# Where the length-47 sets and the token output's quarters stand inside a tile of six channel pairs

## The chip, the cores and the metric

The kernel runs on one core of one Trainium2 chip. The metric is device time in microseconds of one execution, from the first to the last work on the core; the time of a kernel is the median over its runs. All arithmetic is in fp32.

## The reference

For each of 8 batches of 3008 positions and 256 channels, a global filter in the frequency domain comes first, and an MLP-mixer block (token mixing, then channel mixing) after it:

```python
X = np.fft.rfft(x, axis=1)
Y = X * (filt_r + 1j * filt_i)[None, :, :]
y = np.fft.irfft(Y, n=x.shape[1], axis=1)          # (8, 3008, 256)

xt = y.transpose(0, 2, 1)
h = np.maximum(xt @ w_tok1, 0.0) @ w_tok2          # 3008 -> 256 -> 3008
u = y + h.transpose(0, 2, 1)
h2 = np.maximum(u @ w_ch1, 0.0) @ w_ch2            # 256 -> 1536 -> 256
return u + h2
```

## The kernel before, in words

**The filter.** 3008 is 64 x 47. The transform is done in two stages, and back in two. The first stage (length 64) is a run of units over the 47 residues: `a_unit` in its plain form, `a_pair` in the form used from the third group on, which takes sums and differences (`x_sums`) first; its result goes to DRAM (`z_tmp`). The second stage works on 16 *length-47 sets* of two frequencies each: `b_pair` (a product with the table `wb`), `products` (two VectorE instructions that multiply by the filter's real and imaginary parts, straight from PSUM), `join` (two VectorE instructions that add the parts up) and `bi_pair` (the product back), whose result goes to DRAM (`g_tmp`). A set that follows another issues its own `b_pair`, then `bi_pair` of the set before it, then `products`. `b_pair` writes the PSUM banks `acc` and `b`; `bi_pair` writes the two banks `pg`, except for the last set's, which takes `acc` and `b`. After `products`, SP is given the loads for the set two further on (`t2_load`, `w_load`).

The batches go through the filter in groups: batch 0 alone, then (1, 2), (3, 4), (5, 6) and 7. Batch 0's filter runs first. Each other group's filter is woven into the mixer of earlier batches: group (1, 2) beside batch 0, group (3, 4) beside batches 1 and 2, group (5, 6) beside batches 3 and 4, batch 7 beside batches 5 and 6. Batch 7's mixer has no filter work beside it. `dft` is a generator that yields the kind of its next piece: `a` and `w` for first-stage units and the loads after them, `b` for a set, `m` for its join, `i` for the last `bi_pair`.

**The mixer.** `mix` walks over 8 batches x 6 tiles (`m`, 512 positions, the last 448) x 6 channel pairs (`jp`, 0 to 5). One channel pair is called a step here. A step's order on each engine is the program's order:

- TensorE: `up_first` (4 products, L941), then the first part of `down` of the step before (3 products, L975 with `hh`), then token work if any is due; the loop yields *place 0*. `up_last` (3 products, L957); *place 1*. `down`'s second part (2 products, L975 with `t`); *place 1.5*. Its third part (2 products); then `finish` or token work if due; *place 2*. Each fp32 product shows as two TensorE rows.
- VectorE (line L919 is the helper `v`): `up_middle` (`hh`, `s`), one piece of `todo_v` if there is one, `h_sums` of the step before (`t`, three instructions), then the token work's adds, after `up_last` the two `hh` adds, and again one piece of `todo_v`.

Filter pieces are put at the places where `mix` yields. A position is written as 3.2 for channel pair 3, place 2.

`todo_v` holds small VectorE jobs. When a tile's last `down` is issued (step 0 of the next tile, place 2), `finish` puts six there (`a`, `b_`, `c`, `d`, a transpose, a transpose and the store); two run at once and the others at 1.0, 1.1, 2.0 and 2.1. The store is 16 DMAs issued by POOL (L1022). Step 0's `up_first` of the next tile needs `v`, which `v_steps` makes in two jobs (`t13`, `t24`) as soon as that tile's `u` is there.

**The token output.** `u` of the next tile is made one tile ahead. For batch 0, `u_unit` does it in two products (one for each half of the channels). For other batches a seven-product form does it in four *quarters* (`u_quarter`, parts 0 to 3, lines L862 and L840), each in one of the banks `acc` and `b` in turn (`free_bank`); each is read by VectorE adds, and part 0 by a ScalarE copy too. The last part also queues the two `v_steps`, the load of the next weights (`w2m_load`, SP, L881) and lets the next batch's filtered rows be loaded (`t4_load`, SP, L750). The table `own` says at which position each part runs (first entry for batch 0, second for the others); `new`, which is for the last tile, is not touched. At step 32 of a batch the next batch's token sums are made (`token_product`).

**When a filter piece is due.** The main loop asks at each place whether the next piece is due: `a` and `w` at place 1 (three places a step beside batch 0), the rest by tables of positions. With these tables the sets beside batch 0 ran in steps 2, 3 and 5 of tile 1, 1, 2, 3 and 5 of tiles 2 and 3, and 0, 1, 2, 3 and 5 of tile 4, each with its join at place 2 of the same step. Beside later batches a set ran at 5.1.5 and at 2.1.5 (1.1.5 in the last tile), with joins at 0.1 of the next tile and at 3.0.

Of the kernel before, what the change touches and what calls it, by code (L numbers as in the profile page):

```python
# [42 lines left out]
JP = JT // 2  # L43
# [84 lines left out]
def kernel(  # L128
# [299 lines left out]
    def sum_up():  # L428
        while behind:
            behind.pop(0)()  # L430

    def convert():

        convert_middle()
        convert_end()

    def convert_middle():
        advance(middle)
        sum_up()

    def convert_end(copy_now=True):
        ended[0] += 1
        advance(end)
        if copy_now:
            copies()
        fill(5)
# [3 lines left out]
    def copies():  # L450

        while copied[0] < len(tiles) and copied[0] <= ended[0] + 1:
            advance(copy)
            copied[0] += 1
# [3 lines left out]
    def fill(ahead):  # L458
        while not pause and begun[0] < len(tiles) and begun[0] < ended[0] + (4 if begun[0] >= len(tiles) - len(LAST) else ahead):
            start()  # L460

    def start():
        advance(begin)
        begun[0] += 1
# [282 lines left out]
    def t4_load(b, c, lo=PARTS[0], hi=P, queue=nc.sync):  # L747
        if lo == 0:
            t4[b, c] = t4p.tile([P, TC4, D], FP32, tag="t4", name="t4")
        queue.dma_start(t4[b, c][lo:hi], rows_of(g_d, b)[lo:hi, ts(c, TC4), :])  # L750

    def token_sums(b):
        acc = bank(free_bank()).rearrange("p (t d) -> p t d", t=TC)
        for a in range(A):
            for t in range(TC):
                nc.tensor.matmul(acc[:, t, :], w1[:, a, ts(t, P)], t4[b, a // TC4][:, a % TC4, :],
                                 start=(a == 0 and t == 0), stop=(a == A - 1 and t == TC - 1))
        return acc
# [69 lines left out]
    def token_relu(b, acc):  # L828
        h1 = h1p.tile([P, TC, D], FP32, tag="h1", name="h1")
        nc.scalar.activation(out=h1, in_=acc, func=AF.Relu)  # L830
        return h1
# [198 lines left out]
    def u_part(b, m, i):  # L1030
        if i == 0:
            uts[b, m] = up.tile([P, DH, 512], FP32, tag="u", name="u")
        (u_quarter if b else u_unit)(b, m, h1s[b], uts[b, m], i)

    def v_steps(b, m):
        vts[b, m] = vp.tile([P, 4, 256], FP32, tag="v", name="v")
        t13, t2, t4_ = u_sums(uts[b, m], vts[b, m], width(m))

        def t24():
            t2()  # L1040
            t4_()

        return [t13, t24]
# [7 lines left out]
    def mix(next_ready):  # L1051
# [8 lines left out]
                wait.clear()  # L1060


        own = ({(4, 2): (0, 1)}, {(3, 0): (0,), (4, 0): (1,), (4, 2): (2, 3)})
        new = {(JP - 2, 0): (0, 1), (JP - 1, 0): (2, 3)}

        def u_parts(b, m, jp, place):
# [15 lines left out]
        n = MT * JP  # L1082
        for i in range(len(items) + 1):
# [11 lines left out]
            if now:  # L1095
                b, m, jp = items[i]
# [64 lines left out]
    with tc.manual_schedule():  # L1161
        nc.sync.dma_start(wa0, wa0_d)
        nc.vector.memset(turned[:, A:K2, :], 0.0)
        for t in filts:
            nc.vector.memset(t, 0.0)
        half = 0
        second = dft(GROUPS[1])
        for i, _ in enumerate(dft(GROUPS[0])):
            if i == 0:
                nc.scalar.dma_start(wai_t, wait_d)  # L1170
            k = i - NXC - 2

            if i < NXC:
                if i in (1, 3, 5, 7, 9):
                    start()
                if i == NXC - 1:
                    copies()
                    for t, src in ((wa, wa_d), (was, was_d), (wai, wai_d), (ident, ident_d)):
                        nc.scalar.dma_start(t, src)
            elif k >= 0:  # L1180
                if k == K2 - 5:
                    pause.append(True)
                while half < 2 * IN_B * (k + 1) // K2:
                    if half % 2:
                        convert_end()
                    else:
                        convert_middle()
                    half += 1

                if 19 <= k < 25:  # L1190
                    t4_load(0, k - 19, 0, PARTS[1])
                elif 26 <= k < 29:
                    for c in range(2):
                        t4_load(0, 2 * (k - 26) + c, PARTS[1], PARTS[2])
                elif k in (30, 31):
                    for c in range(3):
                        t4_load(0, 3 * (k - 30) + c, PARTS[2], PARTS[3])
        pause.clear()

        fill(5)  # L1200
        for c in range(A // TC4):
            t4_load(0, c, PARTS[3], P, (nc.sync, nc.gpsimd)[c % 2])
        both = wcp.tile([P, 2, JP, 7, P], FP32, tag="wc", name="wc")

        chan.extend((both[:, 0], both[:, 1]))
        next(second)
        for i in range(IN_B, A // 2 + TC * W2G):
            convert()
            if i == A // 2 + BY_PE - 1:
                sum_up()  # L1210
                acc = token_sums(0)

        ahead[0](XF, nc.gpsimd)
        h1s[0] = token_relu(0, acc)
        for dh in range(DH):
            convert()
            u_part(0, 0, dh)
        for f in v_steps(0, 0):
            f()
        convert_end(False)  # L1220
        for _ in range(XB):
            next(second)
        group, todo, done = -1, iter(()), True

        def next_ready(b):
            return done or b != GROUPS[group][-1]

        coming = "a"  # L1230
        n = MT * JP
        for b, i, place in mix(next_ready):
            if group + 1 < len(GROUPS) and b == GROUPS[group + 1][0]:
                if not done:
                    raise AssertionError("the filter's steps don't fit beside the mixer's")
                group += 1
                done = group + 1 == len(GROUPS)
                todo = iter(()) if done else dft(GROUPS[group + 1]) if group else second
                coming = "a"
            if done:  # L1240
                continue
            jp = i % JP
            if coming in "aw":
                due = place == 1 or group == 0 and place != 1.5
            elif group:
                due = (jp, place) in {"b": ((5, 1.5), (1 if i >= n - JP else 2, 1.5)), "m": ((0, 1), (3, 0)), "i": ((1, 0), (3, 2))}[coming]
            else:
                due = (jp - (coming == "i")) % JP in ((5, 1, 2, 3) if i < 4 * JP else (5, 0, 1, 2, 3)) and place == {"b": 1.5, "m": 2, "i": 0}[coming]
            if coming == "a" and group == 0 and i < JP - 1:
                due = {0: 2, 1: 0, 1.5: 0, 2: 1}[place]  # L1250
            for _ in range(due):
                if not done:
                    coming = next(todo, "end")
                    done = coming == "end"
# [30 lines left out]
```

## Time and profile before

| | |
|---|---|
| median of 5 runs | 2460.81 us (2459.18 to 2461.69) |
| profiled execution | 2460.81 us, its span 2459.0 us |
| mean granted TensorE clock | 0.996 |
| busy: TensorE, VectorE, ScalarE, GpSimd (POOL) | 2394.9, 1942.4, 686.4, 619.9 us |
| DMA moved | 278.66 MB, mean 113 GB/s |

Busy time is the union of the instructions of an engine in the one profiled execution. A row of the timeline gives the start in us from the span's start, the duration, the engine, the line of the program, the operation, the tiles it writes and reads, the shape, a count of merged instructions, and in brackets the idle time before it with what ended it. A row of the waits gives who waited for whom: us in total, times, and the longest. A row of the windows gives the stretch, its length, the busy time and instructions of TensorE, its weight loads, VectorE, ScalarE and POOL, then the granted clock, the DMA share and GB/s.

### The profile page before, as it was taken

How to read it: one execution, taken by the hardware profiler on the slowest of the kernel's cores; microseconds unless marked ns; L12 is line 12 of the kernel's file. 1: busy time of each engine (PE TensorE's matmuls, PEld its weight loads, DVE VectorE, ACT ScalarE, POOL GpSimd, SP SyncE). 2: the span in 40 equal slices, each digit the busy share in tenths (PEclk: the TensorE clock that was granted, in tenths of full speed). 3: DMA queues.
4: the chain of work that ended last, by engine and by line, in shares of the span. 5: the costliest groups of instructions: out<-in, count | busy, mean ns of one | idle time of the engine just before them, and what ended most of it. 6: DMA issues, size and time to landing. Idle time of an engine off the chain costs nothing.

```text
span 2459.0 us, 35588 instructions
## 1 busy us (share of the span) xinstructions
PE 2394.9 (97%) x12340; PEld 1979.7 (81%) x12340; DVE 1942.4 (79%) x3684; ACT 686.4 (28%) x1355; POOL 619.9 (25%) x1115
## 2 busy tenths in 40 slices
PE   7999999999999999999999999999999999999998
PEld 4756666978788877987888878897889888898887
DVE  7797788787887788778877887877787788777776
ACT  5733223133222222123222222213221222212222
POOL 7486322122112211211211122112112112112121
PEclk8999999999999999999999999999999999999999
DMA  9985445553442232545333322433324121411100
GB/s 218 243 233 167 155 133 175 161 158 111 116 141 79 82 91 66 171 128 157 92 123 114 92 72 76 160 96 119 96 77 151 46 75 46 146 65 30 39 15 20
DMA packets 187420, 278.66 MB, mean 113 GB/s; under 512 B 35485, under 2 KB 125291, under 8 KB 187240
## 3 DMA queue, kind: packets, MB, share of 16 engines
q1 hardware_dynamic: 140952, 212.56, 28.4%
q0 software_dynamic: 34688, 53.83, 8.1%
q10 hardware_dynamic: 11600, 10.00, 1.3%
q8 instruction: 98, 1.61, 0.3%
q14 instruction: 82, 0.67, 0.1%
HBM read 193.52 MB, written 82.72 MB: 112 GB/s over the span
## 4 chain that ended last, share of the span: by engine, by line
PE 42%; DVE 8%; issue 1%; ACT 0%; SPq 0%; DMA 0%; DVEq 0%; ACTq 0%; POOL 0%
PE ps_po L975 16%; PE ps_pg L941 9%; PE ps_pg L957 6%; PE ps_acc L862 2%; PE ps_b L807 2%; DVE t L919 2%; DVE u L919 2%; PE ps_b L862 1%; PE ps_acc L807 1%; PE ps_b L523 1%; DVE hh L919 1%; DVE s L919 1%; PE ps_pg L523 1%; PE ps_b L840 1%; PE ps_acc L840 1%
## 5 line engine op out<-in xcount | busy, mean ns | idle before, releaser
L1022 POOL DMA_DIRECT2D out_dram<-r x752 | 407.9, 550 | 1653.6 <-ACT hh L962 931.3
L962 ACT ACTIVATE hh<-hh 128x512 f32<-128x512 f32 (+1 forms) x576 | 347.9, 621 | 1086.8 <-DVE hh L919 1086.8
L919 DVE TENSOR_TENSOR hh<-ps_pg,s 128x512 f32<-128x512 f32 (+3 forms) x864 | 482.8, 587 | 212.0 <-ACT s L944 210.9
L975 PE MATMUL ps_po<-t,wc 128*128 128x256 f32 (+1 forms) x2304 | 559.7, 381 | 19.5 <-DVE t L919 18.4
L975 PEld LDWEIGHTS ps_po<-t,wc 128*128 128x128 f32 x2304 | 423.9, 190 | 154.1 <-issue 55.4
L941 PE MATMUL ps_pg<-v,wc 128*128 128x256 f32 (+1 forms) x1728 | 413.5, 375 | 1.4 <-POOL wc L381 1.3
L975 PE MATMUL ps_po<-hh,wc 128*128 128x256 f32 (+1 forms) x1728 | 413.4, 375 | 1.3 <-POOL wc L382 0.8
L941 PEld LDWEIGHTS ps_pg<-v,wc 128*128 128x128 f32 x1728 | 326.8, 190 | 42.2 <-DVE v L919 3.1
L975 PEld LDWEIGHTS ps_po<-hh,wc 128*128 128x128 f32 x1728 | 327.4, 190 | 40.7 <-POOL wc L382 2.0
L957 PE MATMUL ps_pg<-u,wc 128*128 128x256 f32 (+1 forms) x1152 | 294.6, 378 | 5.2 <-DVE hh L919 3.9
L919 DVE TENSOR_TENSOR t<-t,hh 128x256 f32<-128x256 f32 (+1 forms) x576 | 245.8, 427 | 19.8
L957 PEld LDWEIGHTS ps_pg<-u,wc 128*128 128x128 f32 x1152 | 215.4, 190 | 47.4 <-DVE hh L919 22.4
L919 DVE TENSOR_TENSOR s<-ps_pg,hh 128x512 f32<-128x512 f32 (+1 forms) x288 | 196.1, 681 | 30.7 <-DVE hh L919 0.9
L919 DVE TENSOR_TENSOR t<-hh 128x512 f32<-128x512 f32 (+1 forms) x288 | 194.9, 677 | 0.6 <-ACT hh L962 0.6
L944 ACT COPY s<-ps_pg 128x256 f32<-128x256 f32 (+1 forms) x288 | 106.0, 368 | 312.0 <-PE ps_pg L941 309.1
L941 PE MATMUL ps_pg<-u,wc 128*128 128x256 f32 (+1 forms) x576 | 169.9, 377 | 5.2 <-DVE hh L919 5.2
L957 PE MATMUL ps_pg<-v,wc 128*128 128x256 f32 (+1 forms) x576 | 168.8, 375 | 0.0
L941 PEld LDWEIGHTS ps_pg<-u,wc 128*128 128x128 f32 x576 | 107.0, 190 | 25.5 <-DVE hh L919 11.1
L919 DVE TENSOR_TENSOR u<-ps_acc,u 128x256 f32<-128x256 f32 (+1 forms) x84 | 46.2, 550 | 95.3 <-PE ps_acc L862 86.7
L957 PEld LDWEIGHTS ps_pg<-v,wc 128*128 128x128 f32 x576 | 108.7, 190 | 13.1
L919 DVE TENSOR_TENSOR u<-ps_b,u 128x512 f32<-128x512 f32 (+2 forms) x126 | 74.5, 591 | 28.9 <-PE ps_b L862 26.7
L677 DVE TENSOR_TENSOR p<-ps_b,filt 128x1024 f32<-128x1024 f32 (+1 forms) x64 | 69.8, 1091 | 29.8 <-PE ps_pg L523 26.1
(152 smaller groups left out, 2667.7 us busy)
## 6 DMA issues: line engine op xcount, KB each, us to landing
w<-w_tmp SPq DMA_DIRECT2D x84, 448.0 KB
w<-w_tmp SPq DMA_DIRECT2D x35, 896.0 KB
out_dram<-r POOLq DMA_DIRECT2D x696, 32.0 KB, 3.3
t<-g_tmp SPq DMA_DIRECT2D x42, 512.0 KB
g_tmp<-t SPq DMA_DIRECT2D x96, 192.0 KB
t<-z_tmp SPq DMA_DIRECT2D x180, 96.0 KB
z_tmp<-t SPq DMA_DIRECT2D x60, 256.0 KB
filt<-in_x_dram SPq DMA_DIRECT2D x90, 128.0 KB
```

The costliest lines, as they stand in the source:

```text
L523: nc.tensor.matmul(outs(i, j), stat(i, j), mov(i, j), start=True, stop=True)
L677: nc.vector.tensor_tensor(out=prods[c, h], in0=pss[h].unsqueeze(1).to_broadcast([P, 2, nb, D]), in1=filts[c % FB][:, :, 0, :].unsqueeze(2) ...
L807: nc.tensor.matmul(ps[:, at], w[:, n], mov, start=(j == 0 and i in (0, 2)), stop=(j == AP - 1 and i >= 5))
L840: nc.tensor.matmul(ps[:, ds(q * P, n)], t4[b, c][:, r, ts(dh, P)], wai[:, 0:n], start=(first and q == 0), stop=(not first and q == 3))
L862: nc.tensor.matmul(ps[:, ds(j * hw, hw)], h1[:, n, :], w2m[m % 2][:, at, 0:hw], start=(i < 2 and j == 0), stop=(j == len(todo) - 1))
L919: nc.vector.tensor_tensor(out=out, in0=in0, in1=in1, op=op)
L941: nc.tensor.matmul(ps[:, 0:hw], chan[0][:, jp, n, :], mov, start=True, stop=True)
L944: nc.scalar.copy(out=s[:, 0], in_=g[0][:, 0, 0:hw])
L957: nc.tensor.matmul(ps[:, 0:hw], chan[0][:, jp, n, :], mov, start=True, stop=True)
L962: nc.scalar.activation(out=hs, in_=hs, func=AF.Relu)
L975: nc.tensor.matmul(po[i][:, j, 0:hw], chan[1][:, jp, n, :], mov, start=(jp == 0 and first == 1), stop=(jp == JP - 1 and last == 1))
L1022: q.dma_start(bass.AP(tensor=ob.tensor, offset=ob.offset + row * D + g * cw, ap=[[N1 * D, 32], [D if h else -D, n], [1, cw]]), blocks[ts(g ...
```

## The change

Two tables of positions and one condition change; no instruction is added or taken away.

- Sets beside batches 1 to 6 run at 1.1.5 and 4.1.5 of every tile (the second and the fifth channel pair), their joins at 3.1 and 5.1. The last set's way back is due at 0.0 or 3.2.
- Sets beside batch 0 run in steps 2, 3, 4 and 5 of a tile (the third to the sixth channel pair).
- The token output: in batch 0 the two halves run at 3.0 and 4.0, both at 4.2 before. In the others parts 0 and 1 run at 3.0, part 2 at 3.2 and part 3 at 4.0; before, part 0 ran at 3.0, part 1 at 4.0 and parts 2 and 3 at 4.2. So `v_steps` run at 4.1 and 5.0, where they ran at 5.0 and 5.1.

```diff
-        own = ({(4, 2): (0, 1)}, {(3, 0): (0,), (4, 0): (1,), (4, 2): (2, 3)})
+        own = ({(3, 0): (0,), (4, 0): (1,)}, {(3, 0): (0, 1), (3, 2): (2,), (4, 0): (3,)})
...
             elif group:
-                due = (jp, place) in {"b": ((5, 1.5), (1 if i >= n - JP else 2, 1.5)), "m": ((0, 1), (3, 0)), "i": ((1, 0), (3, 2))}[coming]
+                due = (jp, place) in {"b": ((1, 1.5), (4, 1.5)), "m": ((3, 1), (5, 1)), "i": ((0, 0), (3, 2))}[coming]
             else:
-                due = (jp - (coming == "i")) % JP in ((5, 1, 2, 3) if i < 4 * JP else (5, 0, 1, 2, 3)) and place == {"b": 1.5, "m": 2, "i": 0}[coming]
+                due = (jp - (coming == "i")) % JP in (2, 3, 4, 5) and place == {"b": 1.5, "m": 2, "i": 0}[coming]
```

## The prediction

> **What bounds the kernel now.** I read the page first: busy shares, then the waits.
>
> ```profile
> span 2459.0 us, 35588 instructions
> ...
> PE 2394.9 (97%) x12340; PEld 1979.7 (81%) x12340; DVE 1942.4 (79%) x3684; ACT 686.4 (28%) x1355; POOL 619.9 (25%) x1115
> ```
>
> TensorE has work in 97% of the span, and the change neither adds nor removes a matmul. Only idle TensorE time can move: 64.1 us, of which the first 90 us hold 17. TensorE's own waits say for whom it idles later:
>
> ```profile
> PE ps_po L975 <- DVE t L919: 18.4, 36, 0.6
> ```
>
> The matmuls of the down product wait for VectorE's sums t. To see where, I took step lengths from the timeline (start of one first L941 row to the next; a step is one channel pair). Steps 0 to 5 of a tile of batch 7, which has no filter work: 6.12, 6.40, 6.05, 6.90, 9.99, 6.05 us. A tile of batch 2 (from 822.18), with sets in steps 2 and 5: 6.05, 7.15, 8.12, 6.91, 9.99, 8.12. So a set costs 8.12 - 6.05 = 2.07, and step 1, which holds no set, is 0.75 longer than in the bare tile. The windows of the two tiles agree: 46.3 - 41.5 = 4.8, against 2 x 2.07 = 4.14.
>
> ```profile
> 822.20:868.50 46.30, 45.69 (x231) 37.11 (x230) 38.38 (x69) 12.35 (x25) 8.66 (x16) 1.00 0.27 80
> ...
> 2246.90:2288.40 41.50, 41.38 (x199) 36.20 (x199) 31.53 (x62) 10.23 (x21) 8.66 (x16) 1.00 0.13 36
> ```
>
> The timeline of step 1 shows why. First the bare tile (step 1 begins at 2253.06), then the tile with sets (828.23):
>
> ```profile
> 2252.39 0.68 DVE L919 TENSOR_TENSOR u<-ps_po,u 128x512 f32<-128x512 f32 x1
> ...
> 2256.83 0.69 DVE L919 TENSOR_TENSOR t<-hh 128x512 f32<-128x512 f32 x1
> ```
>
> ```profile
> 828.16 0.69 DVE L683 TENSOR_TENSOR p<-p,p 128x512 f32<-128x512 f32 x1
> ...
> 828.76 0.69 DVE L919 TENSOR_TENSOR u<-ps_po,u 128x512 f32<-128x512 f32 x1
> ...
> 832.75 0.68 DVE L919 TENSOR_TENSOR t<-hh 128x512 f32<-128x512 f32 x1
> ...
> 833.58 0.45 PE L975 MATMUL ps_po<-t,wc 128*128 128x256 f32 x1 [0.59 <-DVE t L919]
> ```
>
> The end of a tile (finish: u from ps_po) starts 0.67 before step 1 when VectorE is free, and 0.53 after it when the set's joining (two adds, 0.60 each until the next can start) stands ahead in step 0. t comes 3.77 and 4.52 after step 1's start: the 0.75.
>
> **The change, part by part.** The profiled execution took 2460.81, its span 2459.0 plus 1.8 around it; that is also the median of the five runs (2459.18 to 2461.69). About 0.2% (4.9 us) is what a measurement of this kernel can tell from no change.
>
> *Sets in steps 1 and 4, joins in 3 and 5 (batches 1 to 6).* Step 0 loses its join, so step 1 falls to the bare tile's 6.40 plus the set. A set in step 1 has a row: step 31 of batch 1 (719.0), where the switch to the set and its second half cost 0.10 more than in step 2. Gain per tile with two full sets: 0.75 - 0.10 = 0.65. Is VectorE free by step 0? In step 4 the third quarter's add (0.69) and t13 (0.69) lie before the products (2 x 1.22), which wait for the set's matmuls anyway, about 1.2 later. Products end where the next hh can start (843.84 + 1.21 against 845.03), so step 5 starts undelayed. There t24 (0.43 + 0.43, in a row) now stands before t: hh at 1.53 after the step's start, s to 2.74, t24 to 3.54, t to 4.14, plus 0.14 (833.44 to 833.58) = 4.28, against 4.32 when TensorE gets there. I take 0; bounds: no gain, because t moves later, and 0.7 per tile, from batch 0's step at 384.84 where hh starts 1.2 late. The join in step 5 ends at 7.47; step 0's hh is due at 6.05 + 1.53 = 7.58. Covered.
> Steps 1 with a set before them now: per pair group, batches 1 and 2 (3 and 4 alike): 7.54, 7.16, 8.95 (w 448, set inside) and 7.14, 4 x 7.16. Against 6.40, or 5.98 in the last tile, plus 0.10: 1.03 + 0.65 + 0.78 + 0.65 + 2.6 = 5.7. Two groups: 11.4. The last group has half-width sets (step 1 at 6.62): 0.12 each, 1.1 with its last tile.
> Step 33 of batch 1 (752.2) takes 6.41 and its next 7.13, in batch 2, without a join, 5.30 and 7.02: the join at 3.0 delays the adds that free ps_pg. At 3.1 it follows them, and step 34's quarters cover it: 1.2 + 1.2 + 0.6 = 3.0. But step 35 loses its set, which hid t24 ahead of the next batch's first step (0.25 in batch 3's step 0, 0 in batch 2's): -0.75 for three.
>
> *Quarters 0, 1 at 3.0, 2 at 3.2, 3 at 4.0.* The same 14 rows of L862 and 16 of L840, shifted. The first-stage units (a_pair) beside batches 1, 3 and 5 waited 0.2 for quarter 1's adds in step 4; now they do in step 3: even. Their fetch of w (L881) and of t (L750) moves half a step forward on SP, ahead of a set's loads needed two sets later: nothing. t24 half a step earlier removes the 0.07 at step 0 of five bare tiles: 0.4.
>
> *A price at the last set.* Its second half runs at 3.2 on the banks acc and b (16th set, batches 2, 4, 6). Now quarter 2 precedes it there, and its first bank is quarter 2's: the add on that bank ends 0.2 + 0.69 + 0.13 after the quarter. Against a 0.1 switch: 0.9, three times: -2.7. Bounds: 0 each, if the other bank comes first, and 1.2, if the join's two adds (0.60 each) stand ahead of it.
>
> *A price at the first set.* It moves from step 17 to step 16 of its group (step 10 for the last group): it must be ready at 6.05 + 9.51 + 6.58 = 22.14 after step 14 starts (1172.2). Its inputs are late for a reason that the change leaves alone:
>
> ```profile
> 1179.47 8.66 POOL L1022 DMA_DIRECT2D out_dram<-r  x16 [39.88 <-ACT hh L962]
> 1188.12 1.47 POOL L697 MEMSET filt<- 128x512 f32 x3
> ```
>
> ```profile
> 1188.69 0.33 SPq L226 DMA_DIRECT2D filt<-in_filt_r_dram  x1
> ...
> 1191.62 0.30 SPq L631 DMA_DIRECT2D t<-z_tmp  x1
> ...
> 1195.39 0.36 SPq L632 DMA_DIRECT2D t<-z_tmp  x1
> ```
>
> POOL issues 16 stores before it clears the filter tiles; only then SP issues eight filter loads and eight of t. The DMA windows show the first filter bytes about 1 us after their issue, so I take 1.2 to landing: 1195.39 + 0.36 + 1.2 = 1196.9, wanted by the set's second half at 1194.35 + 0.47. Lost: 2.1; in batches 1 and 5 (last issue at 612.81, 1727.72) 1.2 and 1.3. Sum -4.6; bounds -2 (landing 0.4 after issue) and -8 (whole set waits, landing 1.9).
>
> The Trainium skill speaks against the change more strongly here: "DMA: Bandwidth & Descriptors", section "Anatomy of one DMA — SWDGE (gpsimd) path", gives a DMA a fixed cost of about 2 us. By that an estimate of the three waits is some 2 us higher in all; these SP loads are of the other path, and no row tells the landing of these loads.
>
> *Batch 0: sets in 2, 3, 4, 5, joins in the same steps at place 2; the two token products at 3.0 and 4.0.* Here the join stands before the next hh:
>
> ```profile
> 386.99 0.68 DVE L683 TENSOR_TENSOR p<-p,p 128x512 f32<-128x512 f32 x1
> 387.59 0.42 DVE L919 TENSOR_TENSOR hh<-ps_pg,s 128x256 f32<-128x256 f32 x1
> ...
> 390.05 1.13 PE L975 MATMUL ps_po<-t,wc 128*128 128x256 f32 x4 [0.42 <-DVE t L919]
> ```
>
> A step after a set loses 0.5 to 1.3 unless something fills it. Steps 12 to 17 took 6.50, 9.41, 9.30, 8.71, 11.67, 8.12 = 53.7, where six bare steps, four sets and the token products (5.2) make 49.7: 4.0 lost; 18 to 23 lose 4.4; 24 to 29 lose 7, as a set in step 0 puts its join behind finish (11.44 in step 25); 8 to 11 lose 2.1. Now the products (2.6 each) come before the wait in steps 3 and 4, where TensorE's time covers the join: 0 lost. Step 2 follows a step without a set: 0.05 (step 8). Step 5 meets t24 after a late hh: 1.4 (step 14's 1.2 plus 0.2 for t24 over the transpose). Step 0: 0.5 (step 12); step 1: 1.2 (step 13's without its set). 3.15 a tile, three times, plus 1.5 and 0.3: 11.2 against 17.3. Gain 6; bounds 2 and 9. In tile 0, VectorE is the bound (10.4 of 10.4 us in step 3); half of the token products moves into its shadow: 1.0, bounds 0 and 2.
>
> **Sum.** 11.4 + 1.1 + 3.0 - 0.75 + 0.4 - 2.7 - 4.6 + 6 + 1 = 14.85 less: 2446.0.
>
> **Rivals.**
> 1. *VectorE is late in step 5 and t24 makes it worse* (slower). Mechanism: products from step 4 spill past 1.53 of step 5, then t24 and t follow. It decides when what precedes the products in step 4 grows by over 1.2 us. hh then starts 1.2 late and TensorE waits 1.16 at each of 16 full and about 0.5 at each of 8 half sets: 22.6 lost, 2446.0 + 22.6 = 2468.6. Against it: the rows of step 4 sum to the 1.2 to spare.
> 2. *The wait in step 1 stays*, since the set now stands in step 1 itself (8.95 at step 31 speaks for it, though a join preceded that one): 11.4 and 1.1 fall away, 2458.5, no change.
> 3. *The change in the groups does what it says, and the first set is not late*, since the loads land sooner and POOL's 16 issues end earlier: 4.6 and part of the last set's 2.7 back: 2440.
>
> **How the numbers follow.** Forecast 0.55 (2440 to 2453 by the bounds: batch 0 -4/+3, first sets -3.4/+2.6, step 5 at half its bound for some tiles); rival 3 0.2; rival 2 0.13; rival 1 0.08; anything else slower 0.04. The range 2437 to 2460 takes in rivals 2 and 3 and leaves out rival 1 and a little at each end. Faster: 0.55 + 0.2 + 0.03 of rival 2 = 0.78; same: the 0.1 left of rival 2; slower: 0.08 + 0.04 = 0.12.
>
> **What would show it.** Right: step 1 of batch 2 at 8.5 (6.40 + 2.07 + 0.10) with a hh 1.9 to 2.0 after its start; step 5 at 6.05; the tile 45.7 long; step 16 of batches 1, 3 and 5 with TensorE idle 1 to 2 us before the first set; step 27 of batches 2 and 4 some 0.9 longer. Wrong: rows "PE ps_po <- DVE t" in step 5, or step 1 at 9.2. Batch 0 is right if its steps 3 and 4 take 10.7 each and step 1 about 7.2.

## The result, and the profile after

The changed kernel takes 2456.07 us (median of 23 runs, 2451.14 to 2460.98) where the kernel before took 2461.07 (44 runs, 2458.49 to 2464.03): ratio 0.9978, 95% interval 0.9973 to 0.9984. It is 5.0 us faster; 14.85 was forecast. The profiled execution took 2457.73 us, its span 2456.0. Two of the twelve executions of experiment 6's kernel took 5575 and 14191 us for an unknown reason; its median counts them, its ratio does not.

The page's first lines and TensorE's longest wait, after:

```profile
span 2456.0 us, 35551 instructions
...
PE 2396.7 (98%) x12340; PEld 1987.3 (81%) x12340; DVE 1951.5 (79%) x3684; ACT 686.6 (28%) x1355; POOL 621.0 (25%) x1115
```

```profile
PE ps_po L975 <- DVE t L919: 10.8, 18, 1.6
```

The matmul count is the same, and the wait for t fell from 18.4 to 10.8. Yet busy TensorE time grew by 1.8 us with nothing added: some rows ran at a lower clock. The step lengths place the time. Stages are cut at step starts, and the forecast's terms are put into the stage that each belongs to:

| stage | before | after | change | forecast |
|---|---|---|---|---|
| up to batch 0's step 3 | 169.1 | 171.8 | +2.7 | 0 |
| steps 3 to 7 (first tile) | 50.9 | 54.7 | +3.7 | -1.0 |
| steps 8 to 29 (sets beside batch 0) | 203.0 | 197.7 | -5.3 | -6.0 |
| steps 30 to 35 | 58.0 | 57.9 | -0.1 | 0 |
| batches 1 and 2 | 581.8 | 578.1 | -3.7 | -4.55 |
| batches 3 and 4 | 581.8 | 582.4 | +0.6 | -3.65 |
| batches 5 and 6 | 561.0 | 560.4 | -0.7 | +0.75 |
| batch 7 | 253.4 | 253.0 | -0.4 | -0.4 |

Changes are taken before rounding. The first row is before anything that the change moves: of the kernels below, the ten that leave those steps alone too reached that step between 168.2 and 173.2. So its 2.7 is no effect of the change, and with it the profiled gain is 3.1 where the medians give 5.0.

The steady tiles went as forecast. The windows of the tile of batch 2 from 821.30 and of the bare tile of batch 7, after:

```profile
821.30:867.00 45.70, 45.58 (x231) 37.20 (x230) 38.70 (x69) 12.39 (x25) 8.67 (x16) 1.00 0.29 81
2244.22:2285.65 41.43, 41.31 (x199) 36.23 (x198) 31.63 (x61) 10.24 (x21) 8.67 (x16) 1.00 0.13 36
```

The steps of the first are 6.04, 8.60, 6.04, 9.53, 9.45, 6.04. The timeline of step 1 (from 827.35), VectorE's rows first:

```profile
826.68 0.68 DVE L919 TENSOR_TENSOR u<-ps_po,u 128x512 f32<-128x512 f32 x1
...
831.12 0.68 DVE L919 TENSOR_TENSOR t<-hh 128x512 f32<-128x512 f32 x1
```

```profile
831.95 1.10 PE L975 MATMUL ps_po<-t,wc 128*128 128x256 f32 x4
832.98 0.65 PE L523 MATMUL ps_b<-t,wb 48*64 48x512 f32 x2
```

Finish starts 0.67 before the step, t at 3.77 as in the bare tile, and the down product on t starts with no wait in brackets. The set follows it directly.

Two places did not go as forecast, and a third did. At the first set of batch 3 (step 16 begins at 1185.12) the inputs are late; GpSimd's, SP's and TensorE's rows of the timeline:

```profile
1176.79 8.66 POOL L1022 DMA_DIRECT2D out_dram<-r  x16 [39.87 <-ACT hh L962]
1185.43 1.47 POOL L697 MEMSET filt<- 128x512 f32 x3
```

```profile
1186.00 0.33 SPq L226 DMA_DIRECT2D filt<-in_filt_r_dram  x1
...
1192.87 0.36 SPq L632 DMA_DIRECT2D t<-z_tmp  x1
```

```profile
1193.11 1.43 PE L523 MATMUL ps_b<-t,wb 48*64 48x512 f32 x4 [1.32 <-DMA t<-z_tmp]
1194.38 2.38 PE L523 MATMUL ps_acc<-t,wb 48*64 48x512 f32 x4
1196.68 2.07 PE L975 MATMUL ps_po<-t,wc 128*128 128x256 f32 x4
1198.55 1.06 PE L941 MATMUL ps_pg<-u,wc 128*128 128x256 f32 x2
1199.40 2.43 PE L941 MATMUL ps_pg<-v,wc 128*128 128x256 f32 x6
```

The chain is the one forecast: 16 stores, then the clears, then sixteen loads. But the six L941 rows took 2.43 us; in step 1 of the tile above six such rows took 1.46. The windows over that stretch give the granted clock in the third column from the right:

```profile
1190.00:1192.00 2.00, 1.79 (x9) 1.23 (x7) 1.83 (x4) 0.74 (x2) 0.00 (x0) 1.00 0.32 98
1192.00:1196.60 4.60, 3.49 (x8) 0.85 (x8) 1.64 (x2) 0.48 (x1) 0.00 (x0) 0.77 0.37 108
1196.60:1201.50 4.90, 4.90 (x13) 3.89 (x13) 1.65 (x2) 0.37 (x1) 0.00 (x0) 0.51 0.62 172
1201.50:1210.00 8.50, 8.50 (x41) 7.49 (x40) 7.62 (x15) 1.60 (x3) 0.00 (x0) 1.00 0.66 194
```

The clock records say half speed for 6.8 us from 1194.5. Steps 16 and 17 took 13.43 and 7.43; with inputs in time they take 8.59 and 6.04 (shown below). In batch 1 the same step took 10.51, in batch 5 9.97 (8.16 in time), without a lower clock.

The second place is step 5 of batch 0: 14.88 us, before 8.62. Rows of GpSimd, ScalarE and TensorE:

```profile
188.44 1.11 POOL L766 DMA_DIRECT2D w_tmp<-w  x1
189.55 1.03 POOL L767 DMA_DIRECT2D w_tmp<-w  x1
...
192.16 0.74 ACTq L541 DMA_DIRECT2D z_tmp<-t  x1
```

```profile
200.35 0.59 ACT L539 COPY t<-ps_acc 128x512 f32<-128x512 f32 x1 [5.74 <-DMA z_tmp<-t]
...
201.37 0.37 ACT L944 COPY s<-ps_pg 128x256 f32<-128x256 f32 x1 [0.44 <-ACT t L539]
```

```profile
202.26 2.08 PE L957 MATMUL ps_pg<-u,wc 128*128 128x256 f32 x4 [3.13 <-DVE hh L919]
```

Read upwards: TensorE waits 3.13 us for hh, hh for ScalarE's copy s, and s stands on ScalarE behind a copy of t that waits 5.74 us until earlier writes of z have landed. The clock was halved from 201.2, for 6.8 us. The third place, the last set (step 27 of batch 2), paid about what the forecast gave it (0.79, by experiment 3): 11.11 us, with this row in it:

```profile
989.18 0.65 PE L523 MATMUL ps_acc<-p,wb 64*64 64x512 f32 x2 [0.72 <-DVE u L919]
```

### The profile page after: what moved, and what is told of

It reads as the page before. It is cut to its first block, busy times and chain, and to the rows that moved or that the text cites. A ratio compares the mean times of both kernels' runs of the same rounds, so it can differ in the third digit from the quotient of the medians.

```text
span 2456.0 us, 35551 instructions
## 1 busy us (share of the span) xinstructions
PE 2396.7 (98%) x12340; PEld 1987.3 (81%) x12340; DVE 1951.5 (79%) x3684; ACT 686.6 (28%) x1355; POOL 621.0 (25%) x1115
## 4 chain that ended last, share of the span: by engine, by line
PE 48%; DVE 2%; ACT 0%; issue 0%; SPq 0%; DMA 0%; DVEq 0%; ACTq 0%; POOL 0%
PE ps_po L975 19%; PE ps_pg L941 11%; PE ps_pg L957 8%; PE ps_acc L862 2%; PE ps_b L807 2%; PE ps_b L862 1%; PE ps_acc L807 1%; PE ps_b L523 1%; PE ps_pg L523 1%; PE ps_acc L840 1%; PE ps_b L840 1%; DVE t L919 1%; DVE u L919 1%; DVE hh L919 0%; DVE s L919 0%
## 5 line engine op out<-in xcount | busy, mean ns | idle before, releaser
L975 PE MATMUL ps_po<-t,wc 128*128 128x256 f32 (+1 forms) x2304 | 560.4, 382 | 14.1 <-DVE t L919 10.8
L941 PE MATMUL ps_pg<-v,wc 128*128 128x256 f32 (+1 forms) x1728 | 414.1, 376 | 0.0
L941 PEld LDWEIGHTS ps_pg<-v,wc 128*128 128x128 f32 x1728 | 328.2, 190 | 40.6 <-DVE v L919 2.7
L919 DVE TENSOR_TENSOR t<-t,hh 128x256 f32<-128x256 f32 (+1 forms) x576 | 246.6, 428 | 19.8
L941 PE MATMUL ps_pg<-u,wc 128*128 128x256 f32 (+1 forms) x576 | 169.9, 377 | 2.7 <-DVE hh L919 2.6
L941 PEld LDWEIGHTS ps_pg<-u,wc 128*128 128x128 f32 x576 | 108.5, 190 | 21.6 <-DVE hh L919 5.2
```

Source lines behind the costliest of these rows:

```text
L919: nc.vector.tensor_tensor(out=out, in0=in0, in1=in1, op=op)
L941: nc.tensor.matmul(ps[:, 0:hw], chan[0][:, jp, n, :], mov, start=True, stop=True)
L975: nc.tensor.matmul(po[i][:, j, 0:hw], chan[1][:, jp, n, :], mov, start=(jp == 0 and first == 1), stop=(jp == JP - 1 and last == 1))
```

## Experiments

Each kernel was timed in five rounds beside the kernel before. Steps are read from its profiled execution.

**1. Filter tiles cleared by VectorE** (theory 1: the first sets wait for GpSimd's queue).

```diff
             if not first:
-                nc.gpsimd.memset(filts[c][:, :, 0, :], 0.0)
+                nc.vector.memset(filts[c][:, :, 0, :], 0.0)
```

> Changed kernel, with the filter tiles of the groups from the third on cleared by VectorE where POOL did it behind its 16 stores. Theory 1 (TensorE waits for the first set's loads, and a wait of some 3 us halves its granted clock for 6.8 us more): step 16 of batches 1 and 3 and step 10 of batch 5 fall from 10.5, 13.4 and 10.0 us to 8.6, 8.6 and 8.2, step 17 of batch 3 from 7.4 to 6.0; the granted clock stays 1.0 there; 7 to 10 us less than the changed kernel, about 2447 to 2449. Rival (the loads land late because the DMA engines are busy, not because they are issued late): the steps stay within 1 us of the changed kernel's and the time at 2456.

2453.55 us (ratio 0.9971, 0.996 to 0.9983). Steps 16 of batches 1 and 3 took 8.59 each, step 10 of batch 5 8.16, and no halved clock is left there: batches 1 to 6 went from 578.1, 582.4 and 560.4 to 576.1, 576.7 and 558.4, 9.6 us of the 9.9 that the three first sets had cost. The 2447 to 2449 expected was missed, as 6.1 went back in steps 8 to 29 (203.8 for 197.7), all in step 8: 13.54 for 7.26. Beside batch 0 the edit applies too, and there VectorE comes to the clear at 226.55, where GpSimd had done it at 218.06 to 223.80 in the changed kernel. VectorE's rows of the timeline:

```profile
226.55 1.56 DVE L697 MEMSET filt<- 128x512 f32 x3
236.23 1.22 DVE L677 TENSOR_TENSOR p<-ps_b,filt 128x1024 f32<-128x1024 f32 x1 [3.12 <-DMA filt<-in_filt_r_dram]
```

**2. Batch 0's first tile as before** (theory: the token products hid ScalarE's wait).

```diff
+            if b == 0 and m == 0:
+                parts = {(4, 2): (0, 1)}
             now = parts.get((jp, place), ())
```

> Changed kernel, with the two token products of batch 0's first tile put back at 4.2. Theory 1 (in step 5 ScalarE waits 5.7 us for a z write to land before it can reuse its tile, and the products at 4.2 used to cover that): step 5 falls from 14.9 us to 8.6 and steps 3 to 7 from 54.7 to 51, the halved clock after 201 us is gone; 3 to 6 us less than the changed kernel, 2450 to 2453. Rival (the 3.8 us that the profiled execution lost in tile 0 are chance, as the 2.7 before it are): no difference beyond 1.5 us.

2454.17 us (0.9973, 0.9962 to 0.9984). Steps 3 to 7 took 50.9 for 54.7, step 5 8.62 for 14.88, and the halved clock at 201 is gone. In the profiled execution this undoes the whole 3.7. The median fell by 1.9, short of the 3 to 6 expected, and the intervals do not tell it from 3.7.

**3. The last set's way back at 4.1.5.**

```diff
-... "i": ((0, 0), (3, 2)) ...
+... "i": ((0, 0), (4, 1.5)) ...
```

> Changed kernel, with the last set's way back at 4.1.5 instead of 3.2, so that its bank is no longer the one just written by quarter 2. By the term of the prediction (0.9 us each, measured 0.88 in step 27 of batch 2): 2.7 us less over three groups, 2453.4, step 27 of batch 2 at 9.2 where it was 11.1 and step 28 at 8.4 where it was 7.4. If the next batch's rows, loaded half a step later, come too late for the token product of step 32, that step grows instead.

2454.28 us (0.9971, 0.996 to 0.9982). Steps 27 and 28 of batch 2 took 9.21 and 8.53 for 11.11 and 7.42: 0.79 less, against the 0.9 of the forecast; steps 21 and 22 of batch 6, where the last group's last set ends, lost 0.85.

**4. All three edits.**

> Changed kernel with all three edits: clears on VectorE, batch 0's first tile as before, the last way back at 4.1.5. Theory 1: the three gains add up, 13 to 18 us less than the changed kernel, 2438 to 2443, near the 2446 less its two priced losses (2446 - 4.6 - 2.7 = 2438.7). Rival: the lost microseconds come back elsewhere and the sum stays above 2448.

2447.31 us (0.9947, 0.9935 to 0.996): batches 1 to 6 took 575.7, 575.9 and 557.6, with 13.44 us in step 8 of batch 0 as in 1. That step kept it above the 2438 to 2443 expected.

**5. The wait filled.** Four matmuls whose results are overwritten stand ahead of the first sets, to see whether the halved clock belongs to the wait.

```diff
             pss, wb, t2 = two_banks(turn), wbs[c], t2s[c]
+            if c == 0 and tiled:
+                for i in range(4):
+                    nc.tensor.matmul(pss[i % 2], wai, ..., start=True, stop=True)
```

> The changed kernel with four more matmuls (zeros-to-be-overwritten products of 512 columns each, 256 in the half-width group) ahead of the first set of batches 1, 3 and 5, in the time in which TensorE waits for that set's inputs. Theory A (the wait of about 3 us before the first set of batch 3 halves the granted clock, and that costs more than the wait): the rows show no halved clock near 1194, step 17 of batch 3 goes from 7.43 back to 6.1 and steps 16 and 17 together from 20.9 to 18.5 to 19.5; batches 1 and 5 lose up to 1 us each, as 4 x 0.22 us are added to waits that are nearly covered; median 1 to 2 us under the changed kernel. Theory B (the halved clock is chance or has another trigger): the clock is halved near 1194 all the same, steps 16 and 17 of batch 3 take 20.9 or more, median equal or 1 us over.

2455.08 us (0.9975, 0.9965 to 0.9984). The windows of steps 16 and 17 of batch 3:

```profile
1185.87:1197.89 12.02, 12.02 (x56) 8.24 (x54) 6.62 (x11) 1.60 (x3) 1.78 (x4) 1.00 0.32 84
1197.89:1203.93 6.04, 6.04 (x29) 5.26 (x28) 5.83 (x11) 0.72 (x2) 0.00 (x0) 1.00 0.74 226
```

3.43 us of useless work make the two steps 18.06 long, where the changed kernel's took 20.86. In the three other kernels here whose first sets are late in the same way (2, 3 and the next), the two steps took 18.9, 19.8 and 19.0, each with a stretch of half clock there. Here there is none in the groups. In batch 1 the same matmuls lengthened the two steps from 16.55 to 18.06, so batches 1 to 6 together gained only 0.6 us, and the medians differ by 1.0, inside both intervals. The matmuls also delay the set until all its inputs are there, so that its halves run interleaved:

```profile
1195.90 0.65 PE L523 MATMUL ps_b<-t,wb 48*64 48x512 f32 x2
1195.92 0.65 PE L523 MATMUL ps_acc<-t,wb 48*64 48x512 f32 x2
```

So this shows that the clock stays up without the wait and with the halves together; it does not tell which of the two keeps it up.

**6. The output of w1 issued at step 1**, three steps earlier than in the changed kernel.

```diff
-            if JP - 2 <= i < JP + 2:
+            if i == 1 or JP - 1 <= i < JP + 2:
```

> The changed kernel with the 2.36 MB output of w1 issued three steps earlier in batch 0's first tile (step 1 rather than step 4). Theory A (step 5 of batch 0 takes 14.9 us since ScalarE's copy of t waits for writes of z that queue behind these 2.36 MB): step 5 falls to 8.6 to 9.5, the halved clock at 201 goes away, steps 3 to 7 take 50 to 52 rather than 54.7; a part may come back as a shorter wait in steps 1 to 3; median 2 to 4 us less. Theory B (the wait is VectorE's or ScalarE's own work in that tile): step 5 stays at 14 to 15, median unchanged within 1 us.

2456.51 us (0.998, 0.9972 to 0.9989). Step 5 fell to 9.74, near theory A's 8.6 to 9.5, but step 2 rose from 11.12 to 13.93. ScalarE's row there:

```profile
166.77 0.58 ACT L539 COPY t<-ps_b 128x512 f32<-128x512 f32 x1 [5.33 <-DMA z_tmp<-t]
```

The wait of 5 to 6 us went along with these bytes: it is theirs, and an earlier issue hardly helps (steps 0 to 7 together 83.4 us for 84.3; the median did not fall).

**7. All three edits, GpSimd clearing for the group beside batch 0.** As 4, with this line for the clears:

```diff
+                (nc.vector if tiled else nc.gpsimd).memset(filts[c][:, :, 0, :], 0.0)
```

> The changed kernel with its three losses undone: filter tiles cleared by VectorE in the groups beside batches 1, 3 and 5 only (batch 0's stay on GpSimd), batch 0's first tile with the token products where they were (both halves at 4.2), and the last set's loads, second half and joining where they were (4.1.5). Theory A (the forecast failed by the first sets, the first tile and the last set only; the rest of its sum holds): step 8 of batch 0 back to 7.3, steps 8 to 30 at 197.7, the groups at 575.7, 576 and 558, median 2441 to 2443, that is about 6 under the run with the clears on VectorE everywhere (2447.3). Theory B (VectorE's clears cost in the groups too, or the long waits move elsewhere): 2445 to 2449.

2441.29 us (ratio 0.9919, 0.9906 to 0.9932): 19.8 us under the kernel before, 14.8 under the changed kernel, the best one here. The page and the rows at batch 3's first set:

```profile
span 2439.1 us, 35509 instructions
...
PE 2386.0 (98%) x12340; PEld 1980.9 (81%) x12340; DVE 1956.7 (80%) x3693; ACT 686.4 (28%) x1355; POOL 617.5 (25%) x1106
```

```profile
1168.73 1.56 DVE L697 MEMSET filt<- 128x512 f32 x3
```

```profile
1169.23 8.66 POOL L1022 DMA_DIRECT2D out_dram<-r  x16 [39.86 <-ACT hh L962]
```

```profile
1169.24 0.33 SPq L226 DMA_DIRECT2D filt<-in_filt_r_dram  x1
```

SP's loads now start with the 16 stores and not 9 us after them. Steps 16 and 17 take 8.59 and 6.04, batches 1 to 6 take 575.4, 575.4 and 557.7, and the only stretches of half clock are at the two ends of the span.

**8. Batch 0's part alone** (its sets in steps 2 to 5, its token products at 3.0 and 4.0, in the kernel before).

> The kernel before with batch 0's part of the change alone: sets in steps 2 to 5 and the token products at 3.0 and 4.0. Theory A (the parts add up): steps 3 to 7 take 54.7 (before 50.9), steps 8 to 30 take 197.7 (before 203.0), the batches 1 to 7 as before, median 1 to 2 us under before. Theory B (the gain in steps 8 to 30 needs the other parts of the change): steps 8 to 30 at 201 to 203, median 1 to 4 us over before.

2459.86 us (0.9994, 0.9986 to 1.0003). Steps 3 to 7 took 54.5, steps 8 to 29 197.2, the rest as before: -5.8 and +3.6.

**9. The sets beside batches 1 to 6 alone.**

> The kernel before with the table of sets beside batches 1 to 6 alone (sets at 1.1.5 and 4.1.5, joins at 3.1 and 5.1); the quarters stay at 3.0, 4.0 and 4.2 and batch 0 stays as it was. Theory A (the gain in the groups comes from the join leaving step 0, and needs no moved quarters): step 1 of a full tile of batch 2 at 8.6, steps 4 and 5 together 18.1 (9.99 + 2.07 + 6.05), tile 45.7; no quarter ahead of the last set, so steps 27 and 28 as in the run with the last way back at 4.1.5; the first sets late as in the changed kernel; batches 1 to 6 at 1719 to 1722 us (changed kernel 1720.9, before 1724.6), median 2456 to 2459. Theory B (rival 1 of the forecast: with two quarters behind the set in step 4 VectorE is late in step 5, where t13 and t24 now both stand): steps 4 and 5 together 18.7 to 19.5 in the 24 tiles with sets, median 2468 to 2485, slower than before.

2502.15 us (1.0167, 1.0153 to 1.0181): slower than before by 40.7. Steps 4 and 5 of a tile of batch 2 took 13.84 and 6.04, so step 4 lost 1.8 and step 5 nothing. The waits, and the timeline of step 4:

```profile
PE ps_acc L840 <- DVE p L677: 21.4, 18, 1.6
...
PE ps_b L523 <- DMA t<-z_tmp: 13.2, 3, 4.5
```

```profile
871.78 1.13 PE L975 MATMUL ps_po<-t,wc 128*128 128x256 f32 x4
...
873.09 1.21 DVE L677 TENSOR_TENSOR p<-ps_acc,filt 128x1024 f32<-128x1024 f32 x1
...
874.45 1.13 PE L840 MATMUL ps_acc<-wai,t 128*128 128x128 f32 x8 [1.53 <-DVE p L677]
```

With a set in step 4 and quarters 2 and 3 still at 4.2, the quarter needs a bank that VectorE's products are reading. Theory A fell, and so did B's mechanism, as no step 5 is late, though B's size for the two steps (18.7 to 19.5, measured 19.88) was near. The first sets wait 4.3 to 4.5 us, as step 15 is 2.6 us shorter without two of the quarters and the set is wanted that much earlier; with each such wait the clock was halved for 6.8 us, and step 16 took 19.2.

**10. The quarters alone.**

> The kernel before with the token output's quarters alone moved (0 and 1 at 3.0, 2 at 3.2, 3 at 4.0); the sets stay at 2 and 5 and batch 0 stays as it was. Theory A (the move of the quarters is worth next to nothing by itself): tiles with sets 46.2 to 46.5 as before, the last set's second half at 3.2 pays 0.8 to 0.9 at three places, bare tiles 0.1 less; batches 1 to 7 within 3 us of before, median 2459 to 2464. Theory B (part of the groups' gain is the quarters' own, by t13 and t24 being earlier): tiles of batch 2 at 45.8 to 46.0, median 2453 to 2457.

2465.56 us (1.0015, 1.0006 to 1.0024), 4.1 slower. Tiles with sets take 46.49 (46.33 before); the last set's step pair is the same 11.11 and 7.42 as in the changed kernel. By themselves the quarters cost time.

**11. The kernel before with VectorE's clears in the groups** (the edit of 7 alone).

> The kernel before, with the filter tiles of the groups beside batches 1, 3 and 5 cleared by VectorE and not by GpSimd; nothing else. Theory A (only the changed kernel's earlier first set is late, so only there do earlier filter loads pay): step 17 of batches 1 and 3 stays at 7.26, batches 1 to 6 within 1 us of 1724.6, median within 1.5 us of before. Theory B (earlier loads or a freer GpSimd are worth something in the kernel before too, and the version with three edits owes them that): median 3 to 8 us under before.

2460.89 us (0.9999, 0.999 to 1.0007); batches 1 to 6 within 0.2 each. The kernel before has no late first set, so in the version of 7 VectorE's clears only win back what the change had lost.

## Why the prediction was wrong

**The sum without the terms that experiment 7 undoes came out near.** 14.85 + 4.6 + 2.7 - 1.0 = 21.15 is the forecast with first sets in time, the last set where it was and the first tile left alone. Experiment 7 is that kernel: 2460.81 - 21.15 = 2439.7, measured 2441.3. That it is so near is partly luck: in its stages the last group gained 1.9 more than forecast, batches 1 to 4 0.5 and batch 0 0.7 less.

**Step that failed: the first sets, priced at a loss of 4.6.** They cost 1.9 + 6.2 + 1.8 = 9.9 (in experiments 2, 3 and 6, where they are late too, 10.2, 11.8 and 10.2). The landing of 1.2 us after issue was not the miss: the second half started at 1194.38, 1.15 after the last load's issue ended at 1193.23. Two things were left out. First, when the inputs come one half after the other, the halves run apart and not interleaved: in batch 1 2.25 us (614.30 to 616.55) against 1.02 in time. The rows in time (before), then late (batch 1 after):

```profile
1200.45 0.65 PE L523 MATMUL ps_b<-t,wb 48*64 48x512 f32 x2
1200.46 0.65 PE L523 MATMUL ps_acc<-t,wb 48*64 48x512 f32 x2
...
1201.47 1.13 PE L975 MATMUL ps_po<-t,wc 128*128 128x256 f32 x4
```

```profile
614.30 1.21 PE L523 MATMUL ps_b<-t,wb 48*64 48x512 f32 x4 [0.63 <-DVE v L919]
615.40 1.22 PE L523 MATMUL ps_acc<-t,wb 48*64 48x512 f32 x4
616.55 1.13 PE L975 MATMUL ps_po<-t,wc 128*128 128x256 f32 x4
```

With a start 0.7 late that is its 1.9. Second, the clock: in batch 3 the set starts 1.4 late, running apart costs 1.2, and half clock over the end of the set, the down product (1.87 for 0.97) and step 17 (7.43 for 6.04) the other 3.6. That the fall belongs to the late set is shown by experiment 5, where neither is there; whether the wait or the halves running apart brings it stays open. It was not the same in the four kernels with such sets, one profile of each (here batch 3 for 6.8 us; in 2, 3 and 6 batches 1 and 3 for 3.4 each).

**Step that failed: the first tile, priced at a gain of 1.0.** It cost 3.7. I had VectorE as the bound and asked only what TensorE work would fall into its shadow. The products at 4.2 were themselves a cover, for writes of z that stand behind w1's output; experiment 2 shows the cover, experiment 6 the bytes. The lower clock adds little there: in experiment 3 step 5 took 14.69 without it. The working priced what the products would hide at their new place and never what they hid at the old one. The two misses, 5.3 and 4.7, make 10.0; forecast and median are 9.85 apart.

**Right, or off in size.** Full tiles: 0.65 forecast, 0.63 measured (46.33 to 45.70), step 5 at 6.04 with no wait, so rival 1 did not occur; step 1 at 8.60, so neither did rival 2. Step 33 took 5.30, as forecast. Batch 0's tiles: 5.3 in place of 6; steps 3 and 4 at 10.73 (10.7), step 1 at 7.22 (7.2). The last set: 0.79 in place of 0.9. Half-width tiles: 0.46 each (44.88 to 44.42) in place of 0.12, since such a set costs only 1.2 in step 4 (8.59, and 7.37 in a tile without sets); hence the last group's 1.4 more, although its first set cost 0.5 above its price. Step 1 of batches 2 and 4 took 8.90: 0.3 each was not foreseen. Rival 3, that the first sets are not late, is refuted; the opposite held.

**What rival 1 missed.** It asked what precedes the products in step 4. The gain hangs on what follows them: the parts alone give +40.7, +4.1 and -1.3, together -5.0. With the sets moved, the quarters' move is worth some 44 us (40.7 - 1.3 + 5.0, batch 0's part taken at its own -1.3), since it frees the banks and fills step 15; without them it costs 4.1.

The Trainium skill has a rule for the clock: "TensorE: Matmul & The Clock Gate", section "Why this matters for your kernels", asks for no idle gap of TensorE over some 3 us. The trace agrees for the wait of 3.13 us in the first tile, but in experiment 3 the same place waited 3.07 us at full clock:

```profile
199.83 1.13 PE L957 MATMUL ps_pg<-u,wc 128*128 128x256 f32 x4 [3.07 <-DVE hh L919]
```

In batch 3 TensorE's longest gap before the fall was 1.32 us, and in the kernel before a gap of 1.56 us (at 378.7) left the clock alone. So the length of the wait alone does not decide it here; what else counts was not tested.

## What to carry to other kernels

Before you move work out of a place, ask of its cover as you would of its cost: list every queue that is draining beside it, also those of engines that are far from busy. A late load is priced with what runs after it (at batch 3's first set a gap of 1.3 us went with a loss of 6.2), and removing the cause (here nine microseconds of stores ahead of a clear) is worth more than the wait shows. Parts of a schedule change are not additive: try the companion moves together before dropping one.

## What the runs showed of the hardware

In the thirteen profiles the granted clock fell to half for 3.4 or 6.8 us, each time in or after a wait, and for no other length apart from the ends of a span; at batch 3's first set that was some 3.6 of the 6.2 us lost. Waits of 3.07 us (experiment 3) and 1.56 us (the kernel before) left it at full speed. The 23 runs of the changed kernel spread over 9.8 us, the 44 of the kernel before, whose profile has no such stretch in its middle, over 5.5; that the clock makes the difference was not shown.
